# A fused attention and feed-forward block: output products by pairs of token tiles, operands loaded a block ahead, gates from GpSimd's queue, and a new order of the opening and of the end

## The chip, the cores and the metric

The kernel runs on one core of a Trainium2 chip. A core has five engines, each with its own queue of instructions in a fixed order: TensorE (PE) for matrix products into PSUM, with PEld for the weight loads that run beside it; VectorE (DVE); ScalarE (ACT); GpSimd (POOL); and SyncE (SP), which here only issues DMAs. An engine waits for another by semaphores. The metric is the device time of one execution in microseconds (us), the median of several runs.

## The reference, cut to what matters

```
x: 1 x 2048 x 512, H = 32 heads of Dh = 16, F = 1792, all float32
xn  = layernorm(x)                                   # no scale, no bias
q, k, v = split(xn @ wqkv)
s   = softmax(q k^T * Dh**-0.5) v, heads joined, @ wo
f   = (silu(xn @ w_gate) * (xn @ w_up)) @ w_down
out = x + s * silu(f)
```

## The kernel before, in words

A prologue normalises `x` and makes q, k and v. The attention then runs in 32 **units**: 8 groups of 4 heads times 4 blocks of 512 queries, the last group's four units being 28 to 31. A unit has 16 **key tiles** of 128 keys, which are taken in **blocks** of 2 to 6 tiles. In a block each tile has two slots (n = 0, 1, ...), each a pair of score products for two heads (L906) into `score`, `single` or `spare` banks. ScalarE makes the exponentials out of these banks: one instruction for both halves (L909) or one for each (L916). Some halves are **kept back**: VectorE copies the scores out of the bank (L913), which frees it, and ScalarE makes the exponential in place when the block has ended (L926). The slots so treated are the `shared` list of a block. The value products (`acc`, L428) of a block run as one burst in the next block, behind its first two slots. When a unit's last burst is done, `finish` turns and normalises `acc` (L433 to L453); every second group it writes a quarter of the attention output, `o_d[c, b]`, to DRAM.

TensorE has more to do than attention: between the slots `fill(n)` issues n **fill pairs**, each two products of 64 rows into `bankx` and `banky` (`both`, L242). They come from a queue of generators: the feed-forward work for the four query blocks, then the output projection: three of four quarters for the first two token tiles of block 3 (`project_out(NB - 1, DT - 1)`), then blocks 0, 1 and 2. Each operand is split into a high and a low float32r part (`split_o`, L334 and L335), so a product takes three passes.

`plan()` sets the whole order: a search over (tiles, fill pairs) for each block, by a table of costs (327 a block among them), with a fixed first block (`FIRST`) and a fixed list for the last tiles (`LAST`). `out_steps`, called at the end of each block, starts the loads and splits of the projection's operands, which live in the feed-forward's buffers `hh` and `wd` and go through SP's queue (L351). In the version before, a token tile of a projection takes 12 fill pairs: `bankx` gets the sum over the upper 64 rows, `banky` that over the lower 64. VectorE adds the two (L401, L402), GpSimd multiplies by the gate and adds `x` (L386, L387) and stores (L388). The gates (`g_d`) and `x` come through SP's queue into free parts of `fx` and `gur` (L356, L357). The weights of the projection are split into `fx` (L314, L315); `wdr` is a single buffer for one slice of `w_down`, split by VectorE (L213).

Of the kernel before, what the change touches and what calls it, by code (L numbers as in the profile page):

```python
# [9 lines left out]
F32 = mybir.dt.float32  # L10
# [4 lines left out]
ALU = mybir.AluOpType  # L15
# [4 lines left out]
P = 128  # L20
S = 2048
D = 512
# [3 lines left out]
NB = 4  # L26
TB = S // NB
NT = TB // P
DT = D // P
# [10 lines left out]
DC = D // HALF  # L40
LIMIT = 160.0
SIZES = (2, 3, 4, 5, 6)
LAST = (3, 3, 3, 3, 2, 2)
FIRST = (4, 1, 4, 0, 4, 1, 2, 4, 4)
EARLY = 2


# [14 lines left out]
def plan():  # L62

    ends = [0]
    for i in range(2 * NB):  # L70
        nf = GROUPS[i % 2].stop - GROUPS[i % 2].start
        for n in [3 * DC] * nf + [3 * nf] * NT:
            ends.append(ends[-1] + n)

    ends = [n - ends[1] for n in ends[2:]]
    first = [(4, ends[0])]
    units = H // 4 * NB
    start, stop = sum(k for k, _ in first), (units - 2) * KT
    pace = (ends[-1] - ends[0]) / (stop - start)
    short = lambda k, n: 60 if (k, n) in SHARED else 250 * max(0, 6 * (k - 1) - n)  # L80
    ways = {at: {} for at in range(start, stop + 1)}
    ways[start][ends[0], 4] = 0, None
    for at in range(start, stop):
        room = KT - at % KT
        for (done, last), (cost, _) in ways[at].items():
            rem = next((n for n in ends if n > done), done) - done
            for k in SIZES:
                for n in [rem] + list(range(3, rem - 2)):
                    to = at + k, done + n
                    if not n or n > 6 * k + 6 or k > room or room - k == 1:  # L90
# [3 lines left out]
                    c = cost + 327 + short(k, n) + (120 if k == 6 and n < 24 else 0) + (700 if k == last == 6 and n < 24 else 0) + (650 if n == rem and k == 2 else 0) + abs(n - 4.1 * k) / 2  # L94
# [12 lines left out]
    rest += [3 * DT] * (NT * (NB - 1))  # L107
    parts = []
    for k, n in first + middle + list(zip(pairs[r] + 2 * LAST, rest)):
# [9 lines left out]
def tile_block(ctx: ExitStack, tc: tile.TileContext, x, wqkv, wo, w_gate, w_up, w_down, out):  # L119
    nc = tc.nc  # L120
    ctx.enter_context(tc.manual_schedule())
    x, out = x[0], out[0]
# [21 lines left out]
    banks = (bankx, banky)  # L144
# [95 lines left out]
    def both(lhs, rhs, start, stop):  # L240
        for bank, h in zip(banks, halves):
            mm(bank, lhs[h], rhs[h], start=start, stop=stop)  # L242
# [90 lines left out]
    def split_o(dst, src):  # L333
        dve.tensor_copy(dst[0], src)  # L334
        dve.tensor_sub(dst[1], src, dst[0].bitcast(F32))  # L335

    def load_part():
        for i in range(2):
            pair = two.tile([P, 2, D], F32, tag="gur", name="pair")
            plain.extend(pair[:, j] for j in range(2))  # L340
        for c, tag in enumerate(("gul", "gul", "guh")):
            sp.dma_start(plain[c], o_d[c, NB - 1])
# [4 lines left out]
    def load_out(b, c):  # L347
# [3 lines left out]
        sp.dma_start(parts_o[b, c], o_d[c, b])  # L351
# [10 lines left out]

    def out_steps():
        for b in range(NB - 1):
            if b not in stage and (len(queue) <= NB, 0 in stage and now > stage.get(0, now), ready[0] == DT)[b]:
                for c in range(DT - 1):
                    load_out(b, c)
                stage[b] = now
            if b in stage and b < 2 and (b, 1) not in stage and now > begin[u0 + b]:
                load_out(b, DT - 1)  # L370
# [6 lines left out]
            if (b, 1) in stage and (b, 5) not in stage and now > stage[b, 1]:  # L377
                splits.insert(0 if not b else len(splits), (b, DT - 1))
                stage[b, 5] = now
        for _ in range(min(2, len(splits))):  # L380
            b, c = splits.pop(0)
            split_o(lhs[b, c], parts_o[b, c])
            ready[b] += 1

    def store_out(t, y):
        pool.tensor_mul(y, y, gt[t])  # L386
        pool.tensor_add(xr[t], y, xr[t])  # L387
        (pool if t < end - 1 else sp).dma_start(out[rows[t]], xr[t])  # L388

    def project_out(b, n=DT):  # L390
        catch_up()
        for j in range(NT if n == DT else EARLY):
            t = b * NT + j
            i = 0
            for c in range(n):
                for a, w in ((0, 0), (0, 1), (1, 0)):
                    both(lhs[b, c][a][:, j * P:(j + 1) * P], fx[:, w, c], i == 0, i == 3 * n - 1)
                    i += 1
                    if i == 3 * n and n == DT:
                        y = one.tile([P, D], F32, tag="th", name="y")  # L400
                        dve.tensor_scalar(y, bankx, 0.5, None, op0=ALU.mult)  # L401
                        dve.scalar_tensor_tensor(y, banky, 0.5, y, op0=ALU.mult, op1=ALU.add)  # L402
                        store_out(t, y)
                        if b + 2 < NB:
                            after.append(partial(load_gates, t + NT))
                    elif i == 3 * n:
                        dve.tensor_copy(facc[:, j], bankx)
                        dve.tensor_add(facc[:, j], banky, facc[:, j])
                    yield 3 * n - i

    def load_gate():
        last.extend(on[:3] + [one.tile([P, D], F32, tag="wdr", name="last")])
# [35 lines left out]
    def finish(u, o1=None):  # L448
        g, b = divmod(u, NB)
        normalise(u, 0, TB, o1=o1)  # L450
        if g % 2:
            o2 = late.tile([P, TB], F32, tag="o1", name="o2")
            dve.transpose(o2, on[b])  # L453
            if g < NG - 1 or b < 2:
                (pool if g < NG - 1 else sp).dma_start(o_d[g // 2, b], o2)
            else:
                whole = hh.rearrange("p f j t -> p (f j) t")
                lhs[b, DT - 1] = whole[:, 2 * (DT - 1)], whole[:, 2 * DT - 1]
# [411 lines left out]
    for u in range(units):  # L870
# [3 lines left out]
        for now in range(begin[u], begin[u + 1]):  # L874
# [62 lines left out]
                load_q(u + 1)  # L937
                load_shift(u + 1)
            out_steps()
            if now == begin[units - 1] + 1:  # L940
                load_gate()
            if 0 <= now - begin[units - 1] - 3 < EARLY:
                gate_rest(now - begin[units - 1] - 3)
    values(prev)
    fill(total)
    catch_up()
# [76 lines left out]
```

## Time and profile before

| | us |
|---|---|
| median of 3 runs | 1394.18 (1393.81 to 1394.2) |
| profiled execution | 1393.63 |
| its span | 1391.9 |
| PE busy | 1383.6 (99%) |
| ACT busy | 1155.7 (83%) |
| DVE busy | 772.5 (56%) |
| POOL busy | 89.4 (6%) |
| mean granted TensorE clock | 0.999 |

Rows of a timeline give the start in us from the span's start, the duration, the engine, the line, the operation and `out<-in` by the program's names; in brackets stand the engine's idle time before and what ended it. Rows of the chain of waits give start, duration, engine, first operand and line. The attention proper begins near 156 us, the last feed-forward work ends near 1285, and the last burst of values near 1379.7.

### The profile page before, as it was taken

Reading aid. Unit: us, or ns where it says so; the run is one execution under the profiler, and the core shown is the slowest. Engines: PE = TensorE matmul, PEld = TensorE weight load, DVE = VectorE, ACT = ScalarE, POOL = GpSimd, SP = SyncE. Lnnn points to the kernel's source line nnn. Section 1 sums busy time; section 2 is a strip of 40 time slices with the busy share of each in tenths; the row PEclk is TensorE's granted clock in tenths of the full one; section 3 lists DMA queues with packets and bytes.
Section 4 is the critical chain, followed back from the end, with each engine's and each line's share of the span. In section 5 each row is a group of like instructions: output and inputs, shape, how many; then the busy total and the mean of one; then the engine's idle time right before and its main releaser. Section 6 shows DMA issues by size and latency. Waiting matters only on the chain.

```text
span 1391.9 us, 27666 instructions
## 1 busy us (share of the span) xinstructions
PE 1383.6 (99%) x11197; PEld 863.9 (62%) x11197; DVE 772.5 (56%) x1242; ACT 1155.7 (83%) x1932; POOL 89.4 (6%) x102
## 2 busy tenths in 40 slices
PE   9999999999999999999999999999999999999998
PEld 7788656556555655665556555666556556655554
DVE  6643466355646664565465643665466445655755
ACT  6733588888989898889998988888989888899874
POOL 4200100000000000000000000000000000000344
PEclk9999999999999999999999999999999999999999
DMA  7778541124463511233723402357323311232543
GB/s 241 263 249 269 141 116 44 35 69 112 98 138 81 134 43 36 50 87 87 170 60 109 114 13 51 74 127 152 84 67 94 99 28 47 73 102 85 190 146 108
DMA packets 128693, 149.21 MB, mean 107 GB/s; under 512 B 12593, under 2 KB 80689, under 8 KB 127790
## 3 DMA queue, kind: packets, MB, share of 16 engines
q1 hardware_dynamic: 123246, 126.72, 35.5%
q0 software_dynamic: 4880, 20.12, 3.9%
q8 instruction: 90, 1.47, 0.5%
q10 hardware_dynamic: 432, 0.52, 0.1%
q14 instruction: 45, 0.37, 0.1%
HBM read 107.46 MB, written 40.11 MB: 106 GB/s over the span
## 4 chain that ended last, share of the span: by engine, by line
PE 86%; DVE 2%; ACT 1%; issue 0%; DVEq 0%
PE acc L428 32%; PE bankx L242 29%; PE score L906 9%; PE single L906 8%; PE banky L242 6%; PE spare L906 1%; ACT pr L916 0%; ACT pr L909 0%; PE spare L961 0%; PE banky L961 0%; DVE pr L913 0%; DVE gul L204 0%; DVE wd L335 0%; DVE wd L334 0%; DVE on L446 0%
## 5 line engine op out<-in xcount | busy, mean ns | idle before, releaser
L428 PE MATMUL acc<-pr,vst 128*17 128x512 f32 x4096 | 460.4, 593 | 0.0
L916 ACT ACTIVATE pr<-single 128x512 f32<-128x512 f32 x759 | 427.7, 605 | 19.9 <-PE spare L906 3.1
L909 ACT ACTIVATE pr<-score 128x1024 f32<-128x1024 f32 x327 | 337.1, 1031 | 90.3 <-PE score L906 86.7
L242 PE MATMUL bankx<-fx,guh 64*128 64x512 f32 x896 | 290.3, 392 | 0.1
L242 PE MATMUL banky<-fx,guh 64*128 64x512 f32 x896 | 290.4, 392 | 0.0
L428 PEld LDWEIGHTS acc<-pr,vst 128*17 128x17 f32 x4096 | 114.9, 97 | 277.9 <-issue 273.6
L913 DVE COPY pr<-spare 128x512 f32<-128x512 f32 x185 | 127.9, 691 | 169.0 <-PE spare L906 156.8
L906 PE MATMUL score<-qst,kst 50*128 50x512 f32 x839 | 218.9, 419 | 0.0
L906 PE MATMUL single<-qst,kst 50*128 50x512 f32 x916 | 212.9, 399 | 0.8 <-DVE pr L913 0.7
L242 PE MATMUL banky<-wd,hh 64*128 64x512 f32 x672 | 196.1, 392 | 0.0
L242 PE MATMUL bankx<-wd,hh 64*128 64x512 f32 x672 | 196.0, 391 | 0.0
L926 ACT ACTIVATE pr<-pr 128x512 f32<-128x512 f32 x342 | 187.2, 641 | 1.3 <-DVE pr L913 1.3
L242 PEld LDWEIGHTS bankx<-fx,guh 64*128 64x128 f32 x896 | 166.8, 186 | 21.3 <-DVEq L815 0.6
L242 PE MATMUL bankx<-fx,gul 64*128 64x512 f32 x448 | 175.8, 392 | 0.0
L242 PE MATMUL banky<-fx,gul 64*128 64x512 f32 x448 | 175.5, 392 | 0.0
L906 PEld LDWEIGHTS score<-qst,kst 50*128 50x128 f32 x839 | 98.2, 184 | 118.4 <-ACT pr L916 77.1
L242 PEld LDWEIGHTS banky<-fx,guh 64*128 64x128 f32 x896 | 166.9, 186 | 2.0
L913 DVE COPY pr<-single 128x512 f32<-128x512 f32 x157 | 108.4, 691 | 64.8 <-PE single L906 36.9
L916 ACT ACTIVATE pr<-score 128x512 f32<-128x512 f32 x185 | 111.4, 602 | 34.9 <-PE spare L906 27.5
L242 PEld LDWEIGHTS bankx<-wd,hh 64*128 64x128 f32 x672 | 125.1, 186 | 18.9
L906 PEld LDWEIGHTS single<-qst,kst 50*128 50x128 f32 x916 | 114.0, 184 | 26.5 <-ACT pr L916 8.3
L242 PEld LDWEIGHTS banky<-wd,hh 64*128 64x128 f32 x672 | 125.1, 186 | 5.2
(179 smaller groups left out, 1680.3 us busy)
## 6 DMA issues: line engine op xcount, KB each, us to landing
gur<-in_B_w_gate_dram SPq DMA_DIRECT2D x56, 256.0 KB
gur<-in_B_w_up_dram SPq DMA_DIRECT2D x56, 256.0 KB
wdr<-in_B_w_down_dram SPq DMA_DIRECT2D x56, 256.0 KB
kst<-k_d SPq DMA_DIRECT2D x192, 64.0 KB
qst<-q_d SPq DMA_DIRECT2D x192, 64.0 KB
fx<-xt_d SPq DMA_DIRECT2D x24, 512.0 KB
q_d<-parts SPq DMA_DIRECT2D x16, 512.0 KB
k_d<-parts SPq DMA_DIRECT2D x16, 512.0 KB
```

Of the source, the lines that this page charges most:

```text
L242: mm(bank, lhs[h], rhs[h], start=start, stop=stop)
L428: mm(acc[h * 32:h * 32 + DH + 1], v[:, kt % CT, h * (DH + 1):(h + 1) * (DH + 1)], probs[2 * i + h // 2][:, h % 2], start=kt == 0, stop=kt ...
L906: mm(banked[h], k[r, j, kc * P:(kc + 1) * P], q[r, j], start=True, stop=True)
L909: exps.append(act(pr, both_banks, AF.Exp, scale=0.25))
L913: dve.tensor_copy(pr[:, h], banked[h])
L916: exps.append(act(pr[:, h], banked[h], AF.Exp, scale=0.25))
L926: exps.append(act(part, part, AF.Exp, scale=0.25))
```

## The change

1. **Pairs of token tiles.** A fill pair of a projection now makes one half of the sum for two token tiles: tile 2j in `bankx`, tile 2j + 1 in `banky`. Each bank ends with a whole tile after 24 pairs (18 for the early one). For this, half of each operand lies in the other 64 partitions: `load_pairs` loads it in four DMAs instead of one, and `split_wo` makes a second copy of the weights with its halves exchanged (two DMAs from `fx` into `fx`, a weight slice each).
2. **Evacuation.** One VectorE operation for each tile multiplies bank and gate (L406 of the new file); GpSimd only adds `x`.
3. **Loads.** The operands of block 2 are loaded as soon as those of block 0 are split, and the last quarter of block 2, made in unit 30, goes through DMAs from `o2` into `hh` instead of being split on the spot. Up to four splits (before two) are made at a block's end. Gates live in parts of `facc` and in two buffers of `ga`; from the fifth tile on gates and `x` are loaded through GpSimd's queue.
4. **The end.** The last 32 key tiles go in blocks of `LAST = (5, 5, 6, 4, 6, 6)` with 24 fill pairs each, and the early projection in one block of four tiles.
5. **The opening.** Two halves of the first block (slots 5 and 7) are kept back, its fill pairs stand elsewhere, and a second block of more than four tiles gets a cost of 900.

By `plan()`, as (tiles, fill pairs):

| | before | after |
|---|---|---|
| opening | (4,20) (6,24) (6,24) (4,24) | (4,22) (2,9) (4,15) (6,24) (4,24) |
| end | (2,9) (2,9), then twice (3,12) x4 (2,12) x2 | (4,18) (5,24) (5,24) (6,24) (4,24) (6,24) (6,24) |
| blocks in all | 108 | 102 |

What lies between is unchanged.

ScalarE in the opening, the end of the first block, before:

```order
L909 ACTIVATE pr<-score_8966 128x1024
L916 ACTIVATE pr<-single_8967 128x512
L916 ACTIVATE pr<-single_8968 128x512
L909 ACTIVATE pr<-score_8966 128x1024
L916 ACTIVATE pr<-single_8967 128x512
L916 ACTIVATE pr<-spare 128x512
L269 ACTIVATE th<-bankx 128x512
```

and after:

```order
L925 ACTIVATE pr<-score_8966 128x1024
L932 ACTIVATE pr<-single_8967 128x512
L925 ACTIVATE pr<-score_8966 128x1024
L932 ACTIVATE pr<-spare 128x512
L270 ACTIVATE th<-bankx 128x512
L942 ACTIVATE pr<-pr 128x512 x2
```

One half of slot 5 and one of slot 7 have moved behind the activation `th` that ends the block.

VectorE in the end, before, where block 1's operands (`wd`) are split while tiles of block 0 are evacuated:

```order
L401 TENSOR_SCALAR y<-bankx 128x512
L402 SCALAR_TENSOR_TENSOR y<-banky,y 128x512
L334 CAST wd<-wd 128x512
L335 TENSOR_TENSOR wd<-wd 128x512
L334 CAST wd<-wd 128x512
L335 TENSOR_TENSOR wd<-wd 128x512
L913 COPY pr<-single_8967 128x512
```

and after, at the end of block 0's second pair (`home` is a gate's buffer):

```order
L406 SCALAR_TENSOR_TENSOR home<-bankx,home 128x512
L406 SCALAR_TENSOR_TENSOR home<-banky,home 128x512
L337 CAST wd<-wd 128x512
L338 TENSOR_TENSOR wd<-wd 128x512
L337 CAST hh<-hh 128x512
L338 TENSOR_TENSOR hh<-hh 128x512
L337 CAST hh<-hh 128x512
L338 TENSOR_TENSOR hh<-hh 128x512
L337 CAST hh<-hh 128x512
L338 TENSOR_TENSOR hh<-hh 128x512
L929 COPY pr<-spare 128x512 x2
```

Four splits instead of two now stand between the evacuation and the next kept-back copy.

GpSimd's queue for the first tiles of the projection, before:

```order
L386 TENSOR_TENSOR y<-y,fx 128x512
L387 TENSOR_TENSOR pair<-y,pair 128x512
L388 DMA out_dram<-pair 128x512
L386 TENSOR_TENSOR y<-y,fx 128x512
L387 TENSOR_TENSOR pair<-y,pair 128x512
```

and after, a whole pair of tiles:

```order
L407 TENSOR_TENSOR pair<-facc,pair 128x512
L408 DMA out_dram<-pair 128x512
L407 TENSOR_TENSOR pair<-facc,pair 128x512
L408 DMA out_dram<-pair 128x512
L372 DMA facc<-g_d 128x512
L372 DMA pair<-in_A_x_dram 128x512
L372 DMA facc<-g_d 128x512
L372 DMA pair<-in_A_x_dram 128x512
```

The multiply has gone to VectorE's evacuation, and the four loads for the tiles four further on stand behind the pair's stores.

The core of the diff:

```diff
-LAST = (3, 3, 3, 3, 2, 2)
-FIRST = (4, 1, 4, 0, 4, 1, 2, 4, 4)
+LAST = (5, 5, 6, 4, 6, 6)
+FIRST = (2, 2, 4, 1, 3, 4, 2, 2, 4)
+OPEN = (5, 7)
...
-    rest = [3 * (DT - 1)] * EARLY
-    pairs = {4: (2, 2), 5: (3, 2), 6: (3, 3)}
+    rest = [3 * EARLY * (DT - 1)]
+    pairs = {4: (4,), 5: (5,), 6: (6,)}
...
-    parts[0] = 4, (), list(FIRST[1:])
+    parts[0] = 4, OPEN, list(FIRST[1:])
...
     def split_wo(c):
         dve.tensor_copy(fx[:, 0, c], wor[c])
         dve.tensor_sub(fx[:, 1, c], wor[c], fx[:, 0, c].bitcast(F32))
+        for h in range(2):
+            sp.dma_start(fx[halves[h], :, DT + c].bitcast(F32), fx[halves[1 - h], :, c].bitcast(F32))
...
+    def load_pairs(dst, src, n):
+        for h in range(2):
+            for s in range(2):
+                sp.dma_start(dst[halves[h]].rearrange("p (s j t) -> s p j t", s=2, j=n)[s],
+                             src[halves[s ^ h]].rearrange("p (j h t) -> h p j t", j=n, h=2)[h])
...
-        sp.dma_start(parts_o[b, c], o_d[c, b])
+        load_pairs(parts_o[b, c], o_d[c, b] if src is None else src, 2)
...
-        gt[t] = fx[:, t % NT // 2, DT + t % 2].bitcast(F32)
+        if not homes:
+            homes.extend([facc[:, EARLY + i] for i in range(2)])
+            homes.extend([two.tile([P, D], F32, tag="ga", name="home") for _ in range(2)])
+        gt[t] = homes[t % NT]
         xr[t] = plain[t % NT]
-        sp.dma_start(gt[t], g_d[rows[t]])
-        sp.dma_start(xr[t], x[rows[t]])
+        for dst, src in ((gt[t], g_d), (xr[t], x)):
+            (sp if t < NT else pool).dma_start(dst, src[rows[t]])
...
-        for _ in range(min(2, len(splits))):
+        for _ in range(min(DT, len(splits))):
...
-    def store_out(t, y):
-        pool.tensor_mul(y, y, gt[t])
-        pool.tensor_add(xr[t], y, xr[t])
+    def store_out(t, bank):
+        dve.scalar_tensor_tensor(gt[t], bank, 0.5, gt[t], op0=ALU.mult, op1=ALU.mult)
+        pool.tensor_add(xr[t], gt[t], xr[t])
         (pool if t < end - 1 else sp).dma_start(out[rows[t]], xr[t])
+        if t + NT <= end:
+            after.append(partial(load_gates, t + NT))
...
-                    both(lhs[b, c][a][:, j * P:(j + 1) * P], fx[:, w, c], i == 0, i == 3 * n - 1)
...
+                for s in range(2):
+                    at = (s if n < DT else 2 * s + j) * P
+                    for a, w in ((0, 0), (0, 1), (1, 0)):
+                        both(lhs[b, c][a][:, at:at + P], fx[:, w, DT * s + c], i == 0, i == 6 * n - 1)
...
-                split_o(lhs[b, DT - 1], o2)
-                ready[b] += 1
+                load_out(b, DT - 1, o2)
```

More of the change, by code (lines that the diff above doesn't have):

```diff
@@ L93, in plan @@
                         continue
-                    c = cost + 327 + short(k, n) + (120 if k == 6 and n < 24 else 0) + (700 if k == last == 6 and n < 24 else 0) + (650 if n == rem and k == 2 else 0) + abs(n - 4.1 * k) / 2
+                    c = cost + 327 + short(k, n) + (120 if k == 6 and n < 24 else 0) + (700 if k == last == 6 and n < 24 else 0) + (900 if at == start and k > 4 else 0) + (650 if n == rem and k == 2 else 0) + abs(n - 4.1 * k) / 2
                     if (to[1], k) not in ways[to[0]] or ways[to[0]][to[1], k][0] > c:
                         ways[to[0]][to[1], k] = c, ((at, (done, last)), (k, n))
-    rest = [3 * (DT - 1)] * EARLY
-    pairs = {4: (2, 2), 5: (3, 2), 6: (3, 3)}
+    rest = [3 * EARLY * (DT - 1)]
+    pairs = {4: (4,), 5: (5,), 6: (6,)}
     best = lambda r: min((w[0], key) for key, w in ways[stop - r].items() if key[0] == ends[-1])
@@ L106, in plan @@
         step = ways[step[0][0]][step[0][1]][1]
-    rest += [3 * DT] * (NT * (NB - 1))
+    rest += [6 * DT] * (NT // 2 * (NB - 1))
     parts = []
-    for k, n in first + middle + list(zip(pairs[r] + 2 * LAST, rest)):
+    for k, n in first + middle + list(zip(pairs[r] + LAST, rest)):
         m = 2 * k - 2
@@ L364, in out_steps @@
         for b in range(NB - 1):
-            if b not in stage and (len(queue) <= NB, 0 in stage and now > stage.get(0, now), ready[0] == DT)[b]:
+            if b not in stage and b < 2 and (len(queue) <= NB, 0 in stage and now > stage.get(0, now))[b]:
                 for c in range(DT - 1):
@@ L368, in out_steps @@
                 stage[b] = now
-            if b in stage and b < 2 and (b, 1) not in stage and now > begin[u0 + b]:
-                load_out(b, DT - 1)
+            if b in stage and (b, 1) not in stage and now >= begin[u0 + b]:
+                if b < 2:
+                    load_out(b, DT - 1)
                 stage[b, 1] = now
@@ L376, in out_steps @@
                     load_gates(t)
-            if (b, 1) in stage and (b, 5) not in stage and now > stage[b, 1]:
-                splits.insert(0 if not b else len(splits), (b, DT - 1))
+            if (b, 1) in stage and (b, 5) not in stage and now > stage[b, 1] - b // 2:
+                splits.append((b, DT - 1))
                 stage[b, 5] = now
-        for _ in range(min(2, len(splits))):
+        for _ in range(min(DT, len(splits))):
             b, c = splits.pop(0)
@@ L383, in out_steps @@
             ready[b] += 1
-    def store_out(t, y):
-        pool.tensor_mul(y, y, gt[t])
-        pool.tensor_add(xr[t], y, xr[t])
+        if ready[0] == DT and 2 not in stage:
+            for c in range(DT - 1):
+                load_out(2, c)
+            stage[2] = now
+    def store_out(t, bank):
+        dve.scalar_tensor_tensor(gt[t], bank, 0.5, gt[t], op0=ALU.mult, op1=ALU.mult)
+        pool.tensor_add(xr[t], gt[t], xr[t])
         (pool if t < end - 1 else sp).dma_start(out[rows[t]], xr[t])
+        if t + NT <= end:
+            after.append(partial(load_gates, t + NT))
     def project_out(b, n=DT):
         catch_up()
-        for j in range(NT if n == DT else EARLY):
-            t = b * NT + j
+        for j in range(NT // 2 if n == DT else 1):
             i = 0
             for c in range(n):
-                for a, w in ((0, 0), (0, 1), (1, 0)):
-                    both(lhs[b, c][a][:, j * P:(j + 1) * P], fx[:, w, c], i == 0, i == 3 * n - 1)
[L398 to L409, printed above, removed]
+                for s in range(2):
+                    at = (s if n < DT else 2 * s + j) * P
+                    for a, w in ((0, 0), (0, 1), (1, 0)):
+                        both(lhs[b, c][a][:, at:at + P], fx[:, w, DT * s + c], i == 0, i == 6 * n - 1)
+                        i += 1
+                        if i == 6 * n:
+                            for t, bank in enumerate(banks):
+                                if n < DT:
+                                    dve.tensor_copy(facc[:, t], bank)
+                                else:
+                                    store_out(b * NT + 2 * j + t, bank)
+                        yield 6 * n - i
     def load_gate():
@@ L939, in tile_block @@
             out_steps()
-            if now == begin[units - 1] + 1:
+            if now == begin[units - 1]:
                 load_gate()
-            if 0 <= now - begin[units - 1] - 3 < EARLY:
-                gate_rest(now - begin[units - 1] - 3)
+            if 0 < now - begin[units - 1] <= EARLY:
+                gate_rest(now - begin[units - 1] - 1)
     values(prev)
```

8 lines of the change are left out of this document (4 added, 4 removed).

## The prediction

> **What bounds the kernel now.** I read the busy line first, then the stages, then the chain of waits, and last the engines' own rows in the two places that the change touches.
>
> ```profile
> PE 1383.6 (99%) x11197; PEld 863.9 (62%) x11197; DVE 772.5 (56%) x1242; ACT 1155.7 (83%) x1932; POOL 89.4 (6%) x102
> ```
>
> ```profile
> 200.00:400.00 200.00, 200.00 (x1722) 123.12 (x1722) 108.82 (x169) 175.76 (x297) 1.64 (x3) 1.00 0.36 86
> ...
> 1300.00:1340.00 40.00, 39.92 (x338) 21.88 (x336) 27.95 (x36) 31.42 (x49) 19.19 (x17) 1.00 0.43 137
> ```
>
> The columns behind the length are PE, PEld, DVE, ACT and POOL. TensorE never stops in the middle, at full clock, and ScalarE is 88% busy beside it (175.76 of 200). So only two things can be won: slots that TensorE spends on nothing, and what it spends when it changes from one kind of work to another. The chain of waits shows the second.
>
> ```profile
> 1205.23 5.27 PE acc L428 x48
> 1219.17 5.27 PE acc L428 x48
> ...
> 1317.88 2.70 PE acc L428 x24
> 1320.58 0.43 PE score L906 x2
> 1321.00 0.23 PE bankx L242
> ...
> 1324.73 0.23 PE single L906 x2
> 1324.96 2.70 PE acc L428 x24
> ...
> 1331.59 1.84 PE acc L428 x16
> ```
>
> Each block of key tiles has one burst of value products (acc). Three tiles take 2.70 and two 1.84, so 0.86 a tile and 0.12 to begin; the first score pair behind it takes 0.43 where others take 0.23. From 1321.00 to 1324.73 lie 16 slots (12 fill pairs, 4 score pairs): 0.233 each. A block of 3 tiles and 12 fills needs 3 x 0.86 + 18 x 0.233 = 6.77 and takes 1324.96 - 1317.88 = 7.08: **0.31 us is what a block costs by being one**. A block of 6 and 24 needs 13.55 and takes 1219.17 - 1205.23 = 13.94: 0.39.
>
> **The change, step by step.**
>
> *Fewer blocks at the end.* The number of products is the same (24 fill pairs for two token tiles, before 2 x 12). The last 14 blocks become 7, three of them of 6 and 24. Before 14 x 0.31 = 4.34; after 3 x 0.39 + 4 x 0.31 = 2.41. **Gain 1.9.** This is arithmetic on TensorE's own stream, so it holds as long as nothing else makes TensorE wait.
>
> *Stalls at the end.* These rows of TensorE are the bursts around its two waits there:
>
> ```profile
> 1303.29 2.77 PE L428 MATMUL acc<-pr,vst 128*17 128x512 f32 x24
> ...
> 1310.72 2.77 PE L428 MATMUL acc<-pr,vst 128*17 128x512 f32 x24
> ...
> 1317.81 2.77 PE L428 MATMUL acc<-pr,vst 128*17 128x512 f32 x24
> ...
> 1337.27 1.91 PE L428 MATMUL acc<-pr,vst 128*17 128x512 f32 x16
> ```
>
> ```profile
> 1344.08 0.50 PE L906 MATMUL single<-qst,kst 50*128 50x512 f32 x2 [0.70 <-DVE pr L913]
> 1344.51 1.91 PE L428 MATMUL acc<-pr,vst 128*17 128x512 f32 x16
> ```
>
> 1303.29 to 1310.72 is 7.43 where the same block next takes 7.09: 0.34 lost. 1337.27 to 1344.51 is 7.24 where 2 x 0.86 + 18 x 0.233 + 0.31 = 6.22 is due: 1.02 lost. Both wait for VectorE's copy of a kept-back score half (L913), which stands behind other work in VectorE's order; the first time these:
>
> ```profile
> 1304.73 0.69 DVE L402 SCALAR_TENSOR_TENSOR y<-banky,y 128x512 f32<-128x512 f32 x1
> 1305.34 0.42 DVE L334 CAST wd<-wd 128x512 fp32r<-128x512 f32 x1
> 1305.79 1.69 DVE L335 TENSOR_TENSOR wd<-wd 128x512 fp32r<-128x512 f32 x1
> 1307.40 1.52 DVE L334 CAST wd<-wd 128x512 fp32r<-128x512 f32 x1
> 1308.95 0.69 DVE L335 TENSOR_TENSOR wd<-wd 128x512 fp32r<-128x512 f32 x1
> 1309.56 0.69 DVE L913 COPY pr<-single 128x512 f32<-128x512 f32 x1
> ```
>
> ```profile
> 1305.64 1.28 POOL L386 TENSOR_TENSOR y<-y,fx 128x512 f32<-128x512 f32 x1 [14.56 <-ACT pr L916]
> 1307.01 1.63 POOL L387 TENSOR_TENSOR pair<-y,pair 128x512 f32<-128x512 f32 x1
> ```
>
> A split is 0.42 + 0.69 alone. Beside GpSimd's two operations one half of a split took 1.69 and the next 1.52, so each GpSimd operation held VectorE up by about 1.0. In the new order both places look otherwise: the splits of a pair stand right behind a block's end and the next block's copy is a whole burst of values away; the output of unit 30 no longer passes transpose, split and copy in one run (it goes through a DMA into `hh`, and is split a block's end later). **Gain 1.35.**
>
> *What is late next.* The longest run of the new order is at the end of the second pair: two evacuations, four splits, then the copy of the first kept-back half of a block of 6. Measured from that block's start, the evacuations end at 1.7 (0.3 until the last product is there, 2 x 0.69), four splits take 4.4, and GpSimd's two adds (one for each tile now, no multiply) hold up two or three of the eight halves, 2 to 3 us; the copy is done at about 9.0. TensorE wants that bank at 2 x 0.233 + 0.12 + 5 x 0.86 + 0.43 + 14 x 0.233 = 8.6. **Cost 0.4**; bounds 0 (one half is held up) and 1.4 (one more). At the first pair there are three splits and the first shared half is the block's seventh, so the copy has time. Each tile's evacuation is one operation instead of two, which hides beside the burst in both versions and counts for nothing; that cover ends only if it takes over 4 us.
>
> *The opening.* The first block is bound by ScalarE:
>
> ```profile
> 157.67 1.03 ACT pr L909
> 158.70 0.97 ACT pr L916 x2
> ...
> 165.36 0.50 ACT th L269
> ```
>
> ```profile
> 156.15 0.46 PE L242 MATMUL bankx<-fx,guh 64*128 64x512 f32 x1
> ...
> 165.54 3.63 PE L428 MATMUL acc<-pr,vst 128*17 128x512 f32 x32
> ...
> 174.46 0.39 PE L906 MATMUL score<-qst,kst 50*128 50x512 f32 x1
> ...
> 175.49 0.47 PE L906 MATMUL spare<-qst,kst 50*128 50x512 f32 x1 [0.64 <-issue]
> ...
> 179.16 5.34 PE L428 MATMUL acc<-pr,vst 128*17 128x512 f32 x48
> ...
> 193.26 5.34 PE L428 MATMUL acc<-pr,vst 128*17 128x512 f32 x48
> ```
>
> In the chain ScalarE runs without a gap from 157.67 to 165.86, while TensorE's 34 slots need 7.9 of the 9.39 from 156.15 to 165.54: 1.47 lost. Two half exps of 0.49 (0.97 / 2) now go behind the activation that ends the block, VectorE copies the halves out meanwhile, so ScalarE is 0.97 shorter where TensorE waits for it. **Gain 0.8**; ends 0.5 (scores start two fills sooner, but the first exp does not) and 1.3 (it does, and nearly all comes back). The two exps must be ready 1.7 and 2.6 into the next burst; by the same rows they end 1.5 before that.
>
> The second block (165.54 to 179.16) takes 13.62 where 4 x 0.86 + 36 x 0.233 + 0.39 = 12.22 is due, the third 14.10 where 13.94 is: 1.56 lost, nearly all while a score waits for VectorE, which waits in turn for a weight:
>
> ```profile
> 173.64 0.43 DVE L213 CAST wd<-wdr 128x512 fp32r<-128x512 f32 x1 [0.50 <-DMA wdr<-in_B_w_down_dram]
> ```
>
> Two tiles and then four now stand where six stood, and the weight's wait falls into the burst between them; the extra block costs 0.23 (0.31 + 0.31 + 0.39 against 2 x 0.39). **Gain 1.3**; ends 0.5 and 1.4.
>
> *Loads.* The queue of SP before:
>
> ```profile
> 1282.76 1.76 SPq L351 DMA_DIRECT2D hh<-o_d  x4
> ...
> 1289.15 3.04 SPq L351 DMA_DIRECT2D wd<-o_d  x3
> ```
>
> and the times to landing of GpSimd's:
>
> ```profile
> g_d<-y POOLq DMA_DIRECT2D x16, 256.0 KB, 2.6
> ...
> out_dram<-pair POOLq DMA_DIRECT2D x10, 256.0 KB, 2.3
> ```
>
> Each operand is four DMAs now. From about 1281 SP issues 16 for the first three quarters and the last one, 2 for the turned weights, 8 for gates and x, 12 and 12 for the next two projections. At 0.44 each (1.76 / 4) the first 16 are out by 1288, and their splits come at the end of the first product block, about 1292; the next 22 by 1298 against 1304; the last 12 by 1303 against 1316. At 1.0 each (3.04 / 3, when the DMA engines were full) the first splits would wait. The first row is nearer: the same place, and the gates come behind. Cost 0, hidden by a block's 10 to 12 us. The gates of later tiles go into GpSimd's queue behind that tile's output and are wanted two blocks later, some 24 us; two adds, two stores and four loads with one wait for a landing make some 9 of a pair's 12 us. Cost 0.
>
> A rule that speaks against that last move: the Trainium skill, "SBUF — State Buffer", Who interferes with whom, has VectorE and GpSimd share a port pair under an exclusive lock, and advises to take DMAs off GpSimd's queue, where the lock starves them of descriptors. The held-up splits above (1.69 for 0.69) agree with the lock; that the stores landed after a median of 2.3 speaks against starvation here.
>
> **Sum.** 1.9 + 1.35 - 0.4 + 0.8 + 1.3 = 4.95. The profiled execution took 1393.63 (span 1391.9 and 1.7 around it), so 1388.7; the median of the runs shown, 1394.18, is 0.55 above it, and the median is what is measured: **1389.2**. The tail behind the last burst is unchanged.
>
> **Rivals.**
> 1. *The opening gives nothing*: ScalarE has as many exps to make (two more halves even go alone), and is late in the next block instead. For it: no gap for 8 us. Against: the block behind has room, as this row of ScalarE there shows.
>
> ```profile
> 176.50 0.60 ACT L916 ACTIVATE pr<-single 128x512 f32<-128x512 f32 x1 [0.97 <-PE single L906]
> ```
>
>    Then 2.85 are left: 1391.3. Chance 0.12.
> 2. *VectorE's queue grows too long at the second pair*: more of the eight halves are held up by GpSimd than two or three. Each costs 1.0. Unhindered the copy would be done 1.8 before it is wanted (1.7 + 4.4 + 0.69 against 8.6), so with all eight TensorE waits 6.2 there, and about 1 a pair earlier: 5.35 - 7.2 makes 1.9 slower, 1396.0. It decides from seven halves on. Against: two adds of 1.3 to 1.6 us cannot cover more than about four. Some of it (one to three more, 1390.5 to 1393): 0.08; all: 0.03.
> 3. *Operands land late*, and the end is slower: the second product block's splits need the 38 issues up to the second projection's operands. At q us each, with 3 to land, they are there at 1281 + 38 q + 3; TensorE goes without them until 1309 (end of the first pair's block at 1304, and 5 that the burst and the evacuations cover). At 1.0 this is 13 late: 1402. It decides from q = 0.8, where all of the gain is gone. Against: 0.44 at this place, and four times smaller transfers. Chance 0.07.
> 4. *GpSimd's DMAs are starved*, the lock reaching descriptors: if each of a pair's six takes 2.6 in series, 16 and 3 for adds make 19 of a pair's 12 us; the gates of the last four pairs come 7 us later each, 24 of them covered, some 4 lost: 1393. By the named page's rule this is how it would come out. Chance 0.04.
> 5. *The blocks don't merge in TensorE's order*: excluded, the order has seven bursts fewer at the end and one more at the start.
>
> **How the numbers follow.** My forecast has 0.64, its own range 1388.2 (all ends high: 1.9 + 1.35 + 1.3 + 1.4 = 5.95) to 1390.5 (half way to all ends low, 2.85); rivals 1, 2, 3, 4 have 0.12, 0.11, 0.07, 0.04, unforeseen things 0.02. The range 1387.8 to 1392.2 (0.4 below that for a tail that gets shorter) leaves out some 0.16. Within 0.2% (2.8 us, about what a measurement of this kernel can tell from no change) is 1391.4 to 1397.0. Faster: 0.64, most of rival 1 (0.10), half of the small rival 2 (0.05): 0.79. Slower: most of rival 3 (0.06), unforeseen things and the far end of rival 4 (0.03): 0.09. The rest, 0.12, is within.
>
> **What would show it.** Right: the last seven bursts of values 9.8 to 14 us apart with 0.3 to 0.4 over their slots; no wait of TensorE above 0.2 us before the third burst; the first burst at about 164.7; ScalarE still near 80% busy at the end. Wrong: waits of TensorE for L929 (the copy) or for a split (L337) over 1 us after the second pair; SP's `hh<-o_d` rows at 0.7 or more each; a landing behind VectorE's L406.

## The result: slower, by one wait

The changed kernel takes 1399.88 us in the median of six runs (1396.5 to 1400.19; two near 1396.6, four near 1400), the kernel before 1394.1 (1393.81 to 1394.2): a ratio of 1.0035, 95% interval 1.0022 to 1.0048. The forecast was 1389.2. Two executions far outside all others, 1414.16 of the kernel before and 6502 of run 4's kernel, explain nothing here, but the first widens the intervals of runs 2 to 4 and draws their ratios down, so for these the ratio by medians is given too. The profiled run is one of the shorter ones, 1396.5 with a span of 1394.6, against 1393.63 and 1391.9 before: 2.7 longer.

The busy line and the stage of the end, in the profile of the changed kernel:

```profile
PE 1381.9 (99%) x11197; PEld 871.7 (63%) x11197; DVE 766.5 (55%) x1240; ACT 1156.9 (83%) x1941; POOL 79.7 (6%) x106
```

```profile
200.00:400.00 200.00, 200.00 (x1724) 122.71 (x1724) 108.08 (x166) 176.03 (x297) 1.64 (x3) 1.00 0.37 86
1300.00:1340.00 40.00, 34.29 (x278) 20.93 (x280) 20.98 (x33) 26.36 (x46) 13.11 (x17) 0.91 0.50 153
```

The columns are those of the prediction's rows: length, PE, PEld, DVE, ACT and POOL busy, granted clock, share of the DMA engines, GB/s. The middle is as it was. Between 1300 and 1340 TensorE is busy for 34.29 of 40 us where it was 39.92, at a granted clock of 0.91. TensorE's own rows there show one wait:

```profile
1325.37 0.39 PE L922 MATMUL score<-qst,kst 50*128 50x512 f32 x1
1331.47 0.79 PE L922 MATMUL spare<-qst,kst 50*128 50x512 f32 x1 [5.71 <-DVE pr L929]
```

And it goes on at half speed. Three stretches from the wait on:

```profile
1325.60:1331.60 6.00, 0.29 (x3) 0.13 (x2) 4.80 (x9) 0.85 (x2) 0.00 (x0) 0.75 0.29 114
1331.60:1335.60 4.00, 4.00 (x20) 3.14 (x22) 2.05 (x3) 1.19 (x2) 0.00 (x0) 0.53 0.00 0
1335.60:1339.40 3.80, 3.80 (x37) 2.40 (x37) 2.00 (x4) 3.65 (x7) 0.88 (x1) 1.00 0.02 4
```

Twenty products in 4.0 us, at a clock of 0.53, where 3.8 us hold 37 at full clock: about 1.9 us more. So the wait costs 5.7 + 1.9 = 7.6 in this run; without it the run would have taken 1388.9 by this estimate.

The chain of waits says where the wait comes from:

```profile
1317.18 4.39 DMA qst<-q_d
...
1321.58 0.56 SPq L343
...
1322.18 4.27 DMA wd<-o_d
...
1326.47 0.44 DVE wd L337
...
1327.54 0.43 DVE hh L337
...
1330.73 0.69 DVE pr L929
...
1331.47 0.79 PE spare L922
```

The last quarter of block 1's operand (`wd`, from here on **the quarter**) lands at about 1326.4; VectorE splits it and three operands of block 2 (`hh`), and only then copies the kept-back half that frees TensorE's bank. VectorE's and SP's timelines:

```profile
1317.60 0.68 DVE L406 SCALAR_TENSOR_TENSOR home<-banky,home 128x512 f32<-128x512 f32 x1
1326.47 0.43 DVE L337 CAST wd<-wd 128x512 fp32r<-128x512 f32 x1 [8.19 <-DMA wd<-o_d]
...
1330.73 0.68 DVE L929 COPY pr<-spare 128x512 f32<-128x512 f32 x1
```

```profile
1275.04 16.15 SPq L343 DMA_DIRECT2D hh<-o_d  x16
...
1297.37 9.38 SPq L343 DMA_DIRECT2D wd<-o_d  x12
1307.17 7.65 SPq L343 DMA_DIRECT2D hh<-o_d  x12
1314.91 0.54 SPq L474 DMA_DIRECT2D o_d<-o  x1
1315.54 3.78 SPq L170 DMA_DIRECT2D qst<-q_d  x6
1319.37 0.58 SPq L183 DMA_DIRECT2D qst<-sh_d  x2
1320.00 2.78 SPq L343 DMA_DIRECT2D wd<-o_d  x4
```

The quarter must first be stored (`o_d<-o`) and then loaded again. VectorE had made it before 1305.6, and its store is issued at 1314.91, behind twelve early loads of block 2 at 0.64 each (7.65 / 12); then eight query loads, then its own four. TensorE, VectorE and SP are each in order, and the delay passes through all three.

### The profile page after: what moved, and what is told of

It reads as the page before. It is cut to its first block, busy times and chain, and to the rows that moved or that the text cites. A ratio compares the mean times of both kernels' runs of the same rounds, so it can differ in the third digit from the quotient of the medians.

```text
span 1394.6 us, 27716 instructions
## 1 busy us (share of the span) xinstructions
PE 1381.9 (99%) x11197; PEld 871.7 (63%) x11197; DVE 766.5 (55%) x1240; ACT 1156.9 (83%) x1941; POOL 79.7 (6%) x106
## 4 chain that ended last, share of the span: by engine, by line
PE 86%; DMA 1%; DVE 1%; issue 0%; SPq 0%; DVEq 0%
PE acc L447 32%; PE bankx L243 28%; PE score L922 9%; PE single L922 8%; PE banky L243 7%; PE spare L922 1%; DMA hh<-o_d 0%; DMA qst<-q_d 0%; DMA wd<-o_d 0%; PE spare L977 0%; DVE wd L337 0%; PE banky L977 0%; SPq L343 0%; DVE pr L929 0%; DVE facc L406 0%
## 5 line engine op out<-in xcount | busy, mean ns | idle before, releaser
L925 ACT ACTIVATE pr<-score 128x1024 f32<-128x1024 f32 x318 | 328.0, 1031 | 87.1 <-PE score L922 84.2
L929 DVE COPY pr<-spare 128x512 f32<-128x512 f32 x194 | 134.1, 691 | 182.8 <-PE spare L922 170.6
L942 ACT ACTIVATE pr<-pr 128x512 f32<-128x512 f32 x354 | 193.3, 641 | 0.0
L932 ACT ACTIVATE pr<-score 128x512 f32<-128x512 f32 x194 | 116.9, 603 | 36.0 <-PE spare L922 27.3
L929 DVE COPY pr<-single 128x512 f32<-128x512 f32 x160 | 110.4, 690 | 59.8 <-PE single L922 44.0
```

What stands on the lines that cost most here:

```text
L925: exps.append(act(pr, both_banks, AF.Exp, scale=0.25))
L929: dve.tensor_copy(pr[:, h], banked[h])
L932: exps.append(act(pr[:, h], banked[h], AF.Exp, scale=0.25))
L942: exps.append(act(part, part, AF.Exp, scale=0.25))
```

## Experiments

Four explanations were on the table. **A**: the quarter is late because of its place in SP's queue, and its split, which VectorE must do in order, holds up the copies behind it. **B** (the forecast's "what is late next" and rival 2): four splits ahead of the copy are too many, loads or not. **C**: the DMA engines are full, and everything lands late. **D**: TensorE needs the late operand itself. The last seven blocks of key tiles are called K1 to K7 here: (4,18), (5,24), (5,24), (6,24), (4,24), (6,24), (6,24); the wait is in K4. Block 0, 1 or 2 without a K is the block of queries that a projection belongs to.

**1. The changed kernel once more.** No edit.

> The changed kernel once more, nothing edited. Its runs lie at 1396.5 to 1396.75 and at 1399.8 to 1400.2, and the profile shown is one of the shorter ones, with TensorE waiting 5.71 us at 1325.37. If the late quarter is the whole loss (theory A), a run near 1400 shows the same one wait, longer by 3.4 us to about 9, and nothing else longer by over 0.3. If something else makes the difference (theory C, transfers that slow each other down), the 3.4 us lie spread over several waits or loads.

1399.46. The same single wait, now 8.26 us. VectorE's row for the quarter, and TensorE's last stretch:

```profile
1328.97 0.43 DVE L337 CAST wd<-wd 128x512 fp32r<-128x512 f32 x1 [10.74 <-DMA wd<-o_d]
```

```profile
1335.60:1339.40 3.80, 3.80 (x24) 2.96 (x22) 2.08 (x3) 1.89 (x4) 0.00 (x0) 0.56 0.00 0
```

The quarter came 2.5 later and the half speed lasted longer; no other wait appeared. So in these two profiles the two groups of times are two landings of one transfer.

**2. Block 2's loads behind the quarter's.** The twelve loads go behind the quarter's load in SP's queue, and block 2's three splits from the end of K3 to the end of K4:

```diff
-            if b in stage and (b, 2) not in stage and now > stage[b] and (b < 2 or len(queue) <= 2):
+            if b in stage and (b, 2) not in stage and now > stage[b] + b // 2 and (b < 2 or len(queue) <= 2):
...
-        if ready[0] == DT and 2 not in stage:
+        if ready[0] == DT and 2 not in stage and (1, 1) in stage:
```

> The twelve loads of block 2's first three quarters go into SP's queue behind the load of block 1's last quarter instead of ahead of it, and their splits are made one block's end later (end of the sixth block from the end forward: the (6,24) block of unit 30). Theory A, the queue: block 1's last quarter no longer stands behind twelve issues of 0.64 us, 7.7 us in all; it lands at about 1318.5, when VectorE comes to it at 1318.3. The 5.71 us wait and the 2 us of half speed behind it go: 7.7 off the profiled 1396.5, so 1388.8 (1388 to 1389.6). Theory B, VectorE's four splits alone: one split stands there instead of four, so it too gives about 1389 to 1390. Theory C, traffic of the DMA engines: the same bytes move in the same stretch, the quarter still lands 4 to 8 us late, 1393 to 1400.

1388.85 (1388.46 to 1389.19, 12 runs); ratio to before 0.9954 (0.9930 to 0.9978), by medians 1388.85 / 1393.96 = 0.9963. SP's queue and VectorE in the timeline of this kernel, and TensorE's stretch:

```profile
1307.30 0.33 SPq L474 DMA_DIRECT2D o_d<-o  x1
...
1311.29 2.46 SPq L343 DMA_DIRECT2D wd<-o_d  x4
1313.85 9.30 SPq L343 DMA_DIRECT2D hh<-o_d  x12
```

```profile
1319.48 0.43 DVE L337 CAST wd<-wd 128x512 fp32r<-128x512 f32 x1 [0.64 <-DMA wd<-o_d]
...
1324.61 0.69 DVE L929 COPY pr<-spare 128x512 f32<-128x512 f32 x1 [3.97 <-PE spare L922]
```

```profile
1300.00:1340.00 40.00, 40.00 (x348) 24.53 (x346) 24.89 (x37) 32.63 (x54) 17.75 (x24) 1.00 0.66 188
```

The quarter's split waits 0.64. TensorE no longer waits for the copy; the copy waits for TensorE, which is busy for the whole stretch. C in its strong form falls, since the same bytes move; A and B are both still possible, for one split stands there now and not four.

**3. One DMA an operand.** The halves then lie in other partitions than the products want, so only the time of this kernel means anything. Every other engine has the same work in the same order, the four splits ahead of the copy among it.

```diff
-        load_pairs(parts_o[b, c], o_d[c, b] if src is None else src, 2)
+        sp.dma_start(parts_o[b, c], o_d[c, b] if src is None else src)
```

> Each operand of blocks 0 to 2 comes in one DMA of 128 x 2 KB instead of four of 64 x 2 x 512 B. The halves then don't lie where the pairs want them, so the output of these blocks is another sum; the instructions of every other engine are the same and in the same order, four splits ahead of the copy among them. Theory A: the 44 issues up to block 1's last quarter's store and load become 11 and the quarter lands by 1312; no wait of TensorE over 0.5 us at the end, 1388.8 to 1389.3. Theory B: the splits still stand ahead of the copy, TensorE still waits 4 us or more, 1395 to 1400. Theory C: the same bytes, but in packets of 2 KB; in between.

1388.51 (1388.16 to 1388.86); ratio 0.9952 (0.9925 to 0.9978), by medians 0.9961. From this kernel's timeline, SP's four operands of block 0, and VectorE at the place of the wait:

```profile
1281.14 1.77 SPq L361 DMA_DIRECT2D hh<-o_d  x4
```

```profile
1318.49 1.13 DVE L337 CAST wd<-wd 128x512 fp32r<-128x512 f32 x1
...
1320.27 1.53 DVE L337 CAST hh<-hh 128x512 fp32r<-128x512 f32 x1
...
1324.57 0.68 DVE L929 COPY pr<-spare 128x512 f32<-128x512 f32 x1
```

B falls: four splits, two of their eight halves held up beside GpSimd (1.13 and 1.53 for 0.42), end at 1324.6, and TensorE does not wait. Four operands cost SP 1.77 here; in the changed kernel the twelve DMAs of three cost 7.65.

**4. No copies behind the splits.** K4 keeps no halves back, and its fill pairs are spread evenly over its slots; the queue and the splits are unchanged.

```diff
-        shared, behind = SHARED.get((k, n), ((), even))
+        shared, behind = SHARED.get(len(parts) != 98 and (k, n), ((), even))
```

> The (6,24) block of unit 30 keeps no halves back, so no copy of VectorE stands behind the splits there; SP's queue and the splits are unchanged. Theory A in full (late landing, and an in-order VectorE behind it): TensorE needs the late quarter itself only some 10 fill pairs and 6 score pairs after 1325.4, near 1329, and the quarter is split by 1327.6: the 7.7 us go, and ScalarE's own limit in a block without kept-back halves costs about 1.5 (the kernel's own cost table has 1.5 for it): 1390.3 (1389.5 to 1391.5). If the late operand holds TensorE up by itself (theory D), the wait stays nearly whole: 1394 to 1400.

1390.82 (1390.16 to 1392.71 without the one far outside); ratio 0.9969 (0.9941 to 0.9997), by medians 0.9977. The quarter was as late as in run 1, and TensorE waited for it itself, as the timelines of VectorE and of TensorE show:

```profile
1329.44 0.43 DVE L337 CAST wd<-wd 128x512 fp32r<-128x512 f32 x1 [10.67 <-DMA wd<-o_d]
```

```profile
1329.93 0.50 PE L243 MATMUL bankx<-fx,wd 64*128 64x512 f32 x1 [0.77 <-DVE wd L337]
```

So D is worth 0.8 us here. The rest of the 8.26 that TensorE waited in run 1, with a quarter as late, came from the copies, which have nothing to do with the quarter but stand behind it in VectorE's order.

**5. The opening alone**, on the kernel before:

```diff
-FIRST = (4, 1, 4, 0, 4, 1, 2, 4, 4)
+FIRST = (2, 2, 4, 1, 3, 4, 2, 2, 4)
...
+ (900 if at == start and k > 4 else 0)
...
-    parts[0] = 4, (), list(FIRST[1:])
+    parts[0] = 4, (5, 7), list(FIRST[1:])
```

> The kernel before with the change of the opening alone (first block with two halves kept back and its fill pairs in the new places, the cost of 900 that makes the second block a short one). The end is as before. If the opening is worth what the two profiles say (the fourth block's slots begin at 182.6 instead of 184.4, the last feed-forward work 1.9 earlier), 1394.0 - 1.9 = 1392.1 (1391.8 to 1392.4). If half of that came from elsewhere in the changed kernel, 1393.0.

1392.19 (1391.76 to 1392.43) against 1393.98: 1.8 faster, ratio 0.9987 (0.9978 to 0.9996).

**6. The repaired end alone**: the second kernel with `FIRST`, the first block and the costs of the opening as before.

> The repaired end (as in the run with block 2's loads behind) with the opening of before. If opening and end simply add up: 1388.85 + 1.9 = 1390.75 (1390.4 to 1391.1), so the end alone is worth 3.2. If the end's gain hangs on the opening's order of the feed-forward work, something else.

1390.71 (1390.36 to 1391.38): 3.3 faster, ratio 0.9977 (0.9968 to 0.9987). Opening and end add up: 1.8 + 3.3 = 5.1 = 1393.96 - 1388.85.

**7. Four DMAs of another shape.** As in run 3, only the time counts.

```diff
-        load_pairs(parts_o[b, c], o_d[c, b] if src is None else src, 2)
+        for r in range(0, P, 32):
+            sp.dma_start(parts_o[b, c][r:r + 32], (o_d[c, b] if src is None else src)[r:r + 32])
```

> Four DMAs an operand as in the changed kernel, and in its order, but each of 32 partitions x 2 KB instead of 64 partitions x 2 x 512 B; the halves don't lie where the pairs want them, so the output of blocks 0 to 2 is another sum. If SP's price goes by the number of DMAs (theory A1), each still takes 0.55 to 0.60 and the late quarter stays late: 1396 to 1400. If it goes by the number of packets that a DMA makes, 32 instead of 128 (theory A2), each takes about 0.3, the 44 issues up to the quarter's own are 13 us shorter and nothing is late: 1388.5 to 1389.5.

1390.67 (1390.11 to 1393.82); ratio 0.9981 (0.9972 to 0.9990). SP's sixteen loads of block 0 in the timeline, and VectorE at the quarter:

```profile
1281.17 7.89 SPq L362 DMA_DIRECT2D hh<-o_d  x16
```

```profile
1322.41 0.43 DVE L337 CAST wd<-wd 128x512 fp32r<-128x512 f32 x1 [3.80 <-DMA wd<-o_d]
```

Neither A1 nor A2: 0.49 each (7.89 / 16), against 0.61 to 0.64 for 64 x 2 x 512 B where nothing held the queue up (2.46 / 4 in run 2, 7.65 / 12) and 0.44 for 128 x 2 KB. So most of a DMA's price on SP did not go by its packets or bytes; the finer shape added about a quarter. The quarter came 4 earlier than in the profile of the changed kernel, and TensorE waited 1.30.

**8 and 9. The splits alone.** Eight was to move block 2's splits behind the copies and leave the loads:

```diff
-            if b in stage and (b, 2) not in stage and now > stage[b] and (b < 2 or len(queue) <= 2):
+            if b in stage and (b, 2) not in stage and now > stage[b] + b // 2 and (b < 2 or len(queue) <= 2):
```

> Loads as in the changed kernel; only the three splits of block 2 go one block's end later, so one split stands ahead of the copy instead of four. The quarter of block 1 is as late as before (1326.5, or 1329.0 in the longer runs). Theory A: the copy follows the one split 3 x 1.06 = 3.2 sooner, so TensorE waits 2.7 (5.2) instead of 5.9 (8.4), with 2 to 2.5 of half speed behind it where the wait is long enough: 1396.5 - 3.2 = 1393.3 or less, 1399.8 - 3.2 = 1396.6 in the longer. Theory B, that the number of splits makes the whole loss: 1388.8.

The edit moved nothing: the condition on the queue's length held the splits at K3's end already. It is the changed kernel again: 1399.98 (1399.35 to 1400.68). With `+ b // 2 * 2` the splits do move:

> What the run before this was meant to be: loads as in the changed kernel, and now the three splits of block 2 do stand behind the copies of unit 30's (6,24) block (VectorE: one split, five copies, two evacuations, three splits); every other engine is as in the changed kernel. The late quarter still lands at 1326.5, or 1329.0 to 1329.4. Theory A: the copy comes 3 x 1.06 = 3.2 sooner, so TensorE waits 2.7 to 5.2 instead of 5.9 to 8.4, and is at half speed behind it for 0 to 2.5: 1391.5 to 1393.3 when the quarter lands early, 1396 to 1396.6 when it lands late. Theory B, the number of splits is the whole loss: 1388.8. That VectorE's order does not matter at all: 1396.5 to 1400.

1396.16 (1392.46 to 1398.82); ratio 1.0016 (1.0006 to 1.0025). VectorE in the ninth kernel's timeline:

```profile
1329.51 0.43 DVE L337 CAST wd<-wd 128x512 fp32r<-128x512 f32 x1 [10.63 <-DMA wd<-o_d]
1329.97 0.69 DVE L338 TENSOR_TENSOR wd<-wd 128x512 fp32r<-128x512 f32 x1
1330.58 0.68 DVE L929 COPY pr<-spare 128x512 f32<-128x512 f32 x1
```

3.8 less than run eight by the medians (the two ranges do not overlap); the wait was 4.97 where it was 8.09, 3.1 less, and three splits take 3.2. B has this share: with a late quarter the splits behind it cost what they take, and without one nothing (run 3).

**10. The other half of the repair alone**: the second line of run 2's edit without the first.

> The other half of the repair alone: the loads of block 2 stand behind the quarter's load, but its three splits stay where the changed kernel has them, ahead of the copies. Theory A: the quarter is in time (VectorE comes to it near 1319), but the twelve loads behind it are issued up to 1323.2 and land about 5 later, near 1328; the last split and the copy then end near 1330 and TensorE, which wants the bank at 1325.6, waits about 4, with up to 2 of half speed: 1388.85 + 4 to 6.5 = 1393 to 1395.5. If only the quarter's place counts: 1388.8 to 1389.5.

1395.17 (1389.8 to 1396.2); ratio 1.0004 (0.9994 to 1.0013). VectorE in this kernel's timeline:

```profile
1319.51 0.53 DVE L337 CAST wd<-wd 128x512 fp32r<-128x512 f32 x1 [0.53 <-DMA wd<-o_d]
...
1328.11 0.43 DVE L337 CAST hh<-hh 128x512 fp32r<-128x512 f32 x1 [4.10 <-DMA hh<-o_d]
...
1329.18 0.68 DVE L929 COPY pr<-spare 128x512 f32<-128x512 f32 x1
```

The quarter is in time, block 2's third operand takes its place as the late one, and the copy stands behind that. A load moved back in a queue needs its consumer moved back too.

**11 and 12. Gates in SP's queue**, in the repaired kernel and in the changed one:

```diff
-            (sp if t < NT else pool).dma_start(dst, src[rows[t]])
+            sp.dma_start(dst, src[rows[t]])
```

> The repaired kernel with the gates and x of later tiles in SP's queue again instead of GpSimd's: 16 issues more on SP, 8 of them right behind the twelve loads of block 2 that end at 1323.2. At 0.4 each they are out by 1326.4 and land by about 1331, when the first two are wanted (evacuations at 1330.6). If GpSimd's queue costs nothing and SP's has room here: 1388.85, within 0.4. If GpSimd's queue with its DMAs costs VectorE or the stores something: faster by 0.5 or more. If SP's is too long here: the evacuation waits, and 1389.5 to 1391.

> The changed kernel with block 2's loads where it has them, but the gates and x of later tiles in SP's queue, behind the late quarter's load, instead of in GpSimd's. So SP's queue up to the quarter's load is the same row by row, and GpSimd's four loads of 256 KB (issued 1310.6 to 1313.4) no longer move while it is worked off. If the quarter is late through SP's queue and its order alone (theory A), it lands at 1326.5 to 1329.4 as before: 1396.5 to 1400. If GpSimd's traffic has a part in it (theory C: the DMA engines' share was 1.04 from 1314 to 1320, and the query loads took 4.5 to 5.5 in the changed kernel where they take 3.4 in the repaired one), the quarter's four issues start about 1 to 2 sooner and land in 3 to 4 instead of 4.3 to 5.6: near 1323.5 to 1325, TensorE waits 3 to 4.5, and 1393 to 1395.5.

Repaired: 1388.6 (1388.33 to 1388.88), ratio 0.9963 (0.9948 to 0.9977): the move into GpSimd's queue is worth nothing where nothing is late. Changed: 1392.9 (1391.28 to 1395.27), ratio 0.9994 (0.9984 to 1.0003), 7 less than the changed kernel's median, with no execution as long as its shortest; TensorE still waited 3.62. VectorE there, and the stretch from 1314 to 1320 (the DMA engines' share is the last number but one), of this kernel first and then of the changed one:

```profile
1324.64 0.43 DVE L337 CAST wd<-wd 128x512 fp32r<-128x512 f32 x1 [6.10 <-DMA wd<-o_d]
```

```profile
1314.00:1320.00 6.00, 6.00 (x56) 3.36 (x56) 2.54 (x4) 5.74 (x10) 1.66 (x2) 1.00 0.56 155
```

```profile
1314.00:1320.00 6.00, 6.00 (x58) 3.24 (x58) 2.28 (x4) 5.59 (x10) 1.91 (x3) 1.00 1.04 303
```

So C has its part after all: with GpSimd's four loads the engines were full (1.04 against 0.56), the six query loads ahead of the quarter's took SP 3.78 and in run 1 4.73 instead of 2.71, and the quarter came 2 to 5 us later. Whether that traffic also makes the two groups of times is not shown. Queue place, traffic and VectorE's order each were needed for the full loss; the runs that eased one of them gave back 4 to 11 us of 1400.

The repaired kernel (run 2; run 11 is the same within its spread) beats the kernel before and the changed one.

## Why the prediction was wrong, point by point

- **Fewer blocks, 1.9, and stalls at the end, 1.35: right in sum.** Together 3.25; the repaired end alone is worth 3.3 (run 6) and TensorE waits for nothing in it. No run parts the two terms. Reckoned as in the prediction, the blocks of the repaired end cost 0.3 to 0.4 each.
- **What is late next, 0.4: the mechanism was right, the size 0.** Two halves were held up, the fewer of the two or three assumed, and the copy was ready in time (run 3). This step looked at the very place of the loss, but took the operands for granted.
- **The opening, 0.8 + 1.3: slightly high, 1.8 in all** (run 5). The bursts of values, in the changed kernel, first, third and fourth:

```profile
164.84 3.63 PE L447 MATMUL acc<-pr,vst 128*17 128x512 f32 x32
...
179.06 3.63 PE L447 MATMUL acc<-pr,vst 128*17 128x512 f32 x32
191.44 5.34 PE L447 MATMUL acc<-pr,vst 128*17 128x512 f32 x48
```

  The first comes 0.7 sooner (165.54 before; 164.7 was forecast). The burst within the block behind tile 16 begins at 191.44 where 193.26 stood: 1.8, of which 1.1 behind the first block instead of 1.3. Rival 1, an opening that gives nothing, falls.
- **Loads, cost 0: this step failed.** It was 7.6 us in the shorter profile and 11.0 by the medians (1399.88 - 1388.85). Three things were wrong in it. First, the price of an issue: 0.44 was read off DMAs of 128 x 2 KB and used for DMAs of 64 x 2 x 512 B, which took 0.61 to 0.64 with nothing in the way and up to 0.78 otherwise (9.38 / 12). Second, the count: it set three groups of loads against their own due times ("the last 12 by 1303 against 1316") and did not ask what stands behind those twelve on the same queue: the quarter's store, eight query loads, and the quarter's load. Third, the deadline: the quarter is due not when TensorE multiplies by it (about 1329, run 4) but when VectorE comes to its split (1318.3), since the copies stand behind it. The sign that the prediction had named for being wrong, a wait for L929 of over 1 us after the second pair, is what came. Rival 3 had the mechanism and a chance of 0.07, but worked it out for the second block's first operands, which came in time.
- **The gates in GpSimd's queue, cost 0: right about the stores and gates, wrong about the neighbours.** They were not late themselves; they took the DMA engines from the query loads and the quarter (run 12). Of starvation (rival 4) nothing was seen: with the same loads in SP's queue the repaired kernel takes as long (1388.6 against 1388.85, run 11). What the queues share is the engines. The Trainium skill says as much in "DMA: Bandwidth & Descriptors", Rules for kernel authors: DMAs from several queues run on the same 16 engines, so spreading them saves only issue time. The trace agrees: the loads of GpSimd's queue raised the share of the same engines from 0.56 to 1.04.
- **The sum**: 4.95 forecast, 5.1 measured with the queue repaired, so 1389.2 was a good forecast for the kernel of run 2. Some of that is luck: the end was forecast 0.4 too low (2.85 against 3.3) and the opening 0.3 too high (2.1 against 1.8). In the range, half way to all ends low is 1390.3 and not 1390.5; nothing hangs on it.

## What to carry to other kernels

When loads are moved ahead, write down the whole queue from there to the next thing that must round-trip through it (a store and its load back), at the price of the new shape, and not only the moved loads' own deadlines. An operand is due when the in-order engine that prepares it comes to it, if anything on the critical path stands behind that. Prefetch belongs behind what is due sooner, and its consumers must stay behind it.

## What the runs showed of the hardware that was not expected

- A long wait of TensorE costs more than its length. After waits of 3.44 us (run 10), 3.62 (run 12), 4.97 (run 9), 5.71 and 8.26 it worked on at a granted clock of 0.50 for 3.4 to 5.2 us, half of which, some 2 us, is lost; after 0.77 (run 4) and 1.30 (run 7) the clock stayed at 1.00. The Trainium skill, "TensorE: Matmul & The Clock Gate", Part 1, puts the limit at an idle window of about 3.4 us and the warm-up at as much. The lengths of these waits fit that, but the moment does not, as three stretches of run 10 show:

```profile
1326.30:1328.20 1.90, 0.18 (x1) 0.00 (x0) 0.09 (x1) 0.86 (x2) 0.00 (x0) 1.00 0.95 372
1328.30:1335.00 6.70, 5.08 (x24) 4.06 (x26) 3.95 (x7) 1.79 (x3) 0.00 (x0) 0.50 0.01 4
1335.10:1337.00 1.90, 1.90 (x18) 1.50 (x17) 0.49 (x2) 1.65 (x3) 0.00 (x0) 1.00 0.00 0
```

  TensorE's last product before that wait ends at 1326.48, so the clock fell 1.8 us into it; in the changed kernel it fell 2.8 us in. In these traces the half clock lasted 3.4 us (run 12), 6.8 (the changed kernel, runs 9 and 10) or 10.2 (runs 1 and 8), whole multiples of 3.4. Waits between 1.30 and 3.44 at this place were not seen, so where between them the loss sets in stays open.
- SP's price for an issue goes with its shape: 0.44 (128 x 2 KB), 0.49 (32 x 2 KB), 0.61 to 0.64 (64 x 2 x 512 B); splitting an operand in four made it nearly six times dearer on the queue (7.65 / 3 = 2.55 against 1.77 / 4 = 0.44). The Trainium skill, "DMA: Bandwidth & Descriptors", Rules for kernel authors, advises to join small transfers and says that under 64 KB most is overhead; here, at 64 KB, four DMAs cost SP nearly six times what one of the same bytes does.
